# A retention block followed by a low-rank mixer and MLP: the first MLP layer of the last two tiles partly as seven half-size products

## The chip, the cores and the metric

The kernel runs on one core of a Trainium2 chip. The metric is the device time of one execution in microseconds; the time of a kernel is the median of several executions. TensorE (PE in the profile) multiplies matrices into PSUM, VectorE (DVE) and ScalarE (ACT) read PSUM and work element by element, GpSimd (POOL) works on SBUF only, SyncE (SP) and POOL issue transfers.

## The reference

Eight sequences of 576 tokens go through a retention (linear attention with a decay per head, 8 heads of 64), and its output `x` (8 x 576 x 512) through a token mixer of rank 32 and an MLP of width 2048:

```python
scores = scale * np.matmul(q, k.transpose(0, 1, 3, 2))
ret = scores * Dmat[None]                     # gamma_h ** (i - j) for i >= j, else 0
x = np.matmul(ret, v)                         # heads side by side: (8, 576, 512)
h = x.transpose(0, 2, 1) @ U @ V
u = x + h.transpose(0, 2, 1)
out = u + np.maximum(u @ w_ch1, 0.0) @ w_ch2  # w_ch1: 512 x 2048, w_ch2: 2048 x 512
```

Only `np.maximum(u @ w_ch1, 0.0)`, the first layer, is what the change touches.

## The kernel before

The 4608 tokens are cut into nine tiles of 512 for the MLP. While tile j goes through the MLP, the retention and the mixer of sequence j+1 are worked in between its pieces; tiles 7 and 8, the last two, have nothing beside them, since the sequences have run out. Each engine executes its instructions in the order in which the program issues them (every engine object is wrapped in `Pinned`, which keeps program order), so a waiting instruction holds up all that stands behind it on its engine.

`mlp_units(j)` gives a tile's pieces, called units, and they are issued in order.

The first layer has 16 units, one for each of the `NF` blocks of 128 rows of the hidden layer. `first(f)` takes a PSUM bank from `ps_mm` (three banks in turn) and issues four matmuls of 128 x 512 that add up over the 512 inputs: weights from `w1_sb`, moving data from `ring["uT"]`, the transposed `u` of the tile's four chunks of 128 tokens. `relu(f)` on ACT writes the bank as bf16 into `y1` (16 blocks x 512 tokens). From tile 2 on the blocks are visited in the order 0, 8, 1, 9, ..., so that a block of the first half (`f < 8`) and its partner in the second half come together.

The second layer of tiles 2 to 8 is already done in seven products of half size (Strassen's scheme in Winograd's form), 14 units of eight matmuls of 128 x 256 each: `products` lists them, `product(n, half)` issues them. `quarter(i, fh)` is the part of `y1` with token half `i` and hidden half `fh`. The scheme needs sums of the quarters (`sum_up`, `difference`, `last_sum`, all on DVE, into `y1_sums` or in place) and sums of the quarters of the second weight (`w2_sums`, made once). `GROUPS` says after which units of the first layer `sum_up` takes two blocks of each half. The products share three PSUM banks "a", "b" and "c", taken from the same `ps_mm`. The functions `after_1`, `after_6`, ... add the products up and add `u`: `after_1` copies bank "a" on ACT; `after_6` adds bank "b" on DVE and then issues three additions of `u` on POOL, the first of which makes the output quarter `22` and the second the quarter `21`; `after_7` adds banks "b" and "c" to quarter `22`, stores it, and calls `last_sum`; `after_2` adds `u` to bank "a" on DVE and stores; `after_4` and `after_3` add banks "b" and "c" to the last two quarters. Product number 5 (counted from 0) adds onto bank "b" that `after_7` has read, and product number 6 reads what `last_sum` wrote.

The loop that issues all tiles but the first ends so:

```python
for n, unit in enumerate(units1 if j == 1 else mlp_units(j)[0]):
    while steps and steps[0][0] <= n:
        steps.pop(0)[2]()
    if j > 1 or n >= 3:
        unit()
for s in steps:
    s[2]()
```

Buffers that are no longer used in the last two tiles are the retention's: `k_sets` and `v_sets` (three each), `q_raw` (two), and the PSUM pools `banks["one"]` (three banks, tag "att") and `banks["two"]` (one buffer of two banks, tag "pss").

Of the kernel before, what the change touches and what calls it, by code (L numbers as in the profile page):

```python
# [8 lines left out]
FP32 = mybir.dt.float32  # L9
BF16 = mybir.dt.bfloat16  # L10
AF = mybir.ActivationFunctionType
ALU = mybir.AluOpType
# [55 lines left out]
def kernel(  # L68
# [12 lines left out]
    pe = Pinned(tc, nc.tensor)  # L81
    dve = Pinned(tc, nc.vector)
    act = Pinned(tc, nc.scalar)
# [6 lines left out]
    R = moe_U.shape[1]  # L90
    P = 128
# [4 lines left out]
    NF = dff // P  # L96
# [5 lines left out]
    NT = B * S // 512  # L102
# [19 lines left out]
    CH = 64  # L122
# [12 lines left out]
    ps_mm = ctx.enter_context(tc.tile_pool(name="ps_mm", bufs=3, space=bass.MemoryType.PSUM))  # L135
    banks = {}
# [6 lines left out]
    q_raw = [consts.tile([P, NR_COLS], BF16, name=f"q_all{i}") for i in range(NQ)]  # L143
# [15 lines left out]
    k_sets = [consts.tile([P, NB, H, D], BF16, name=f"k_all{i}") for i in range(NSET)]  # L159
    v_sets = [consts.tile([P, NB, H, D], BF16, name=f"v_all{i}") for i in range(NSET)]  # L160


    HF, HD = NF // 2, dm // 2
# [41 lines left out]
    w1_sb = consts.tile([P, NCC, dff], BF16, name="w1_sb")  # L205
# [94 lines left out]
    def clear_pads(b):  # L300
        m, pad = (NB - 1, slice(HALF, P)) if b % 2 == 0 else (0, slice(0, HALF))
        for x in (k_sets, v_sets):
            pool.memset(x[b % NSET][pad, m, :, :], 0.0)
# [245 lines left out]
    def mix_turn_by_dma(a, n):  # L549
# [8 lines left out]
    ring = {  # L558
        "u": consts.tile([P, NRING, dm], BF16, name="u_t"),
        "uT": consts.tile([P, NRING, NCC, P], BF16, name="uT_t"),  # L560
    }
# [351 lines left out]

    GROUPS = {4: (0, 2), 8: (2, 4), 12: (4, 6), 15: (6, 8)}

    def sums_of_w2(part):

        f = slice(part * HF // 2, (part + 1) * HF // 2)
        (b11, b12), (b21, b22) = (
            [w2_sb[:, fh * HF:(fh + 1) * HF, q * HD:(q + 1) * HD][:, f, :] for q in range(2)]  # L920
            for fh in range(2)
        )
        t3, t2, t4 = (w2_sums[:, i, f, :] for i in range(3))
        for to, x, y, op in (
            (t3, b22, b12, ALU.subtract), (t2, t3, b11, ALU.add), (t4, b21, t2, ALU.subtract),
        ):
            dve.tensor_tensor(out=to, in0=x, in1=y, op=op)

    def last_sum_of_w2(part):
        f = slice(part * HF // 2, (part + 1) * HF // 2)  # L930
        x = w2_sb[:, 0:HF, HD:dm][:, f, :]
        dve.tensor_tensor(out=x, in0=x, in1=w2_sb[:, 0:HF, 0:HD][:, f, :], op=ALU.subtract)

    def mlp_units(j):
        held = {}
# [6 lines left out]
        own = 4 * j % NRING  # L942
        sums = j >= 2
        order = [f for i in range(HF) for f in (i, i + HF)] if sums else list(range(NF))

        def relu(f):
            act.activation(out=y1()[:, f, :], in_=held.pop(f), func=AF.Relu)
# [10 lines left out]
        def first(f):  # L958
            held[f] = ps = ps_mm.tile([P, 512], FP32, tag="mm", name="ps_y1")
            for cc in range(NCC):  # L960
                pe.matmul(
                    ps, w1_sb[:, cc, f * P:(f + 1) * P], ring["uT"][:, own:own + 4, cc, :],
                    start=(cc == 0), stop=(cc == NCC - 1),
                )

        def second(i, part):
            if part == 0:
                held["out", i] = ps_mm.tile([P, 512], FP32, tag="mm", name="ps_y2")
            for f in range(4 * part, 4 * part + 4):
                pe.matmul(  # L970
                    held["out", i], y1()[:, f, i * P:(i + 1) * P], w2_sb[:, f, :],
                    start=(f == 0), stop=(f == NF - 1),
                )

        def add_and_store(i):
            o_sb = osb_pool.tile([P, dm], FP32, tag="o_sb", name="o_sb")
            dve.tensor_tensor(
                out=o_sb, in0=held.pop(("out", i)), in1=ring["u"][:, own + i, :], op=ALU.add
            )
            t0 = (4 * j + i) * P  # L980
            sp.dma_start(out=out.rearrange("b s d -> (b s) d")[t0:t0 + P, :], in_=o_sb)
# [19 lines left out]
        def sum_up(a, z):  # L1001

            f = slice(a, z)
            s1, s2 = (y1_sums[:, i, f, :] for i in range(2))
            dve.tensor_tensor(
                out=s1, in0=quarter(1, 0)[:, f, :], in1=quarter(1, 1)[:, f, :], op=ALU.add
            )
            dve.tensor_tensor(out=s2, in0=s1, in1=quarter(0, 0)[:, f, :], op=ALU.subtract)

        def difference(a, z):  # L1010
            f = slice(a, z)
            x = quarter(1, 0)[:, f, :]
            dve.tensor_tensor(out=x, in0=quarter(0, 0)[:, f, :], in1=x, op=ALU.subtract)
# [78 lines left out]
        def product(n, half):  # L1092
            bank, fresh, left, right, after = products[n]
            if bank not in held and rows_apart(bank):
                held[bank] = [
                    banks["one"].tile([P, 2, HD], FP32, tag="att", name="ps_y2") for _ in range(2)
                ]
            if bank not in held:
                held[bank] = ps_mm.tile([P, 2, HD], FP32, tag="mm", name="ps_y2")
            apart = rows_apart(bank)  # L1100
            for f in range(HF):
                pe.matmul(
                    bank_rows(bank, half), left()[:, f, half * P:(half + 1) * P],
                    right()[:, f, :], start=(fresh and (apart or half == 0) and f == 0),
                    stop=(f == HF - 1), skip_group_check=True,
                )
            if j == NT - 1 and after is after_3:
                after_3_rows(half)
            elif half == 1 and after:
                after()  # L1110

        def unit(n, alone=True):

            i, part = divmod(n - NF, 4)
            if n < NF:
                first(order[n])
            elif sums:
                product(*divmod(n - NF, 2))
            else:
                second(i, part)  # L1120
            if alone and n < NF:
                relu(order[n])
                if sums and n in GROUPS:
                    sum_up(*GROUPS[n])
                if sums and n == NF - 1:
                    difference(0, HF // 2)
                    difference(HF // 2, HF)
            elif alone and part == 3 and not sums and not (j == 1 and i in (1, 2)):
                add_and_store(i)

        steps = {"y": ahead, "R": relu, "M": lambda n: unit(n, False), "O": add_and_store}
        return [lambda n=n: unit(n) for n in range(NF + (14 if sums else 16))], steps


# [128 lines left out]
    n = 16  # L1263
    while n < SP:
        m = min(n, SP - n)
        dve.tensor_scalar(
            out=iota_col[:, n:n + m], in0=iota_col[:, 0:m], scalar1=float(n), scalar2=None,
            op0=ALU.add,
# [7 lines left out]
    for h in range(H):  # L1276
# [6 lines left out]
        out=ident, in_=ident, compare_op=ALU.not_equal, fill=1.0, base=0,  # L1283
# [13 lines left out]
    for i in range(2):  # L1297
# [7 lines left out]
        out=maskbin, in_=maskbin, compare_op=ALU.is_ge, fill=0.0, base=0,  # L1305
# [27 lines left out]
    for h in range(H):  # L1333
        dve.tensor_scalar(
            out=masks[:, h, :, :], in0=mask64, scalar1=float(gammas[h] ** -CH), scalar2=None,
            op0=ALU.mult,
# [6 lines left out]
            tc.tile_pool(name="ps_" + name, bufs=n, space=bass.MemoryType.PSUM))  # L1343


    for j in range(1, NT):
        if j == 1:
            clear_pads(4)
        steps = []
        if j == 1:  # L1350
            steps = sorted(
                attention_steps(2, (5, 8.5, 12, 15.5, 21), 1.5, 22, 8) + late
                + [(at, 3, lambda i=i: sums_of_w2(i)) for i, at in enumerate((3.2, 21.5))],
                key=lambda s: s[:2]
            )
        elif j + 1 < B:
            last = 17 if j < 5 else 16
            steps = attention_steps(j + 1, (-1.5, 2.5, 6.5, 10.5, last), 1.5, last + 1.8)
        if j == 2:
            steps += [(at, 3, lambda i=i: last_sum_of_w2(i)) for i, at in enumerate((2, 3))]  # L1360
        if 1 < j and j + 2 < B:
            wait_for_turns(j)
            load_for_turns(j + 2)
            if j + 3 < B:
                clear_pads(j + 3)
        if j + 2 < B:
            at = 22 if j == 1 else 20
            steps += [(at + h, 4, lambda h=h: scale_head(j + 2, h)) for h in range(H)]
        steps.sort(key=lambda s: s[:2])
# [4 lines that stand above are left out]
                unit()  # L1374
        for s in steps:
            s[2]()

# [28 lines left out]
```

## Time and profile before

| | |
|---|---|
| median of three executions | 314.66 us (313.89 to 316.91) |
| the profiled execution | 315.51 us, its span 313.8 us |
| granted TensorE clock | 0.993 |
| PE busy | 305.6 us, 97% of the span |
| DVE busy | 229.0 us, 73% |
| ACT busy | 166.8 us, 53% |
| POOL busy | 131.3 us, 42% |

A profile describes one execution; its time beyond the span (1.7 us here) lies before the first and after the last instruction. The timeline view lists, by start, how long a merged run of equal instructions lasted, on which engine, output <- inputs, shapes, count, and in brackets the idle time of the engine just before it with what ended it. The view of groups gives count, total busy time and mean duration in ns. Every instruction carries line L25, the helper's, so it is told apart by the names of its tiles: `ps_y` is any PSUM bank of the MLP, `w_sb` both weights, `uT_t` the transposed `u`, `y_t` the hidden layer, `y_sums` its sums, `kv_runs` the sums of the second weight, `o_sb` an output quarter on its way to memory. PE durations include the drain of the pipeline, so the rate of matmuls is read from the distances of their starts.

### The profile page before, as it was taken

The page shows a single profiled execution, that of the slowest core. Times are in us where ns is not written, and L with a number is a line of the kernel's source. Part 1 is how long each engine was busy: PE and PEld are TensorE (multiplying, and loading weights), DVE is VectorE, ACT ScalarE, POOL GpSimd, SP SyncE. Part 2 cuts the span into 40 slices and gives each one's busy share as a digit, 9 for nine tenths or more (in the row PEclk, how much of TensorE's full clock was granted, in tenths as well). Part 3 has the DMA queues.
Part 4 walks back from the last instruction along what each step waited for, and adds up shares of the span by engine and source line. Part 5 has one row for each costly group of instructions (what it writes and reads, how often), then busy time and mean ns, then how long its engine had stood idle before and what let it go on. Part 6 is the DMA issues. An engine that isn't in the chain of part 4 may idle for free.

```text
span 313.8 us, 9434 instructions
## 1 busy us (share of the span) xinstructions
PE 305.6 (97%) x3937; PEld 190.9 (61%) x3952; DVE 229.0 (73%) x562; ACT 166.8 (53%) x346; POOL 131.3 (42%) x171
## 2 busy tenths in 40 slices
PE   8799999999999999999999999999999999999995
PEld 3575446745544557855784578457845784685484
DVE  6776818877988997899688968996799772352245
ACT  7556605447725775377437745774377406604610
POOL 8492258849302952259439612961200120040040
PEclk9979999999999999999999999999999999999999
DMA  7999999999995999799999994999910052002003
GB/s 117 193 182 198 204 212 145 170 184 133 173 123 162 158 113 146 118 157 148 154 210 162 143 148 119 178 139 118 212 56 4 3 131 86 2 33 102 0 2 135
DMA packets 154523, 40.58 MB, mean 129 GB/s; under 512 B 139088, under 2 KB 153456, under 8 KB 154480
## 3 DMA queue, kind: packets, MB, share of 16 engines
q0 software_dynamic: 91344, 17.09, 71.7%
q1 hardware_dynamic: 63136, 22.88, 40.9%
q8 instruction: 31, 0.51, 0.7%
q14 instruction: 12, 0.10, 0.1%
HBM read 36.85 MB, written 9.44 MB: 147 GB/s over the span
## 4 chain that ended last, share of the span: by engine, by line
PE 84%; DVE 7%; DMA 4%; issue 2%; SPq 1%; ACT 0%; POOL 0%; DVEq 0%; POOLq 0%
PE ps_y L25 69%; PE xh L25 5%; PE ps_b L25 4%; DMA given<-in_v_dram 2%; DMA kv_runs<-in_v_dram 2%; PE sc L25 2%; SPq L25 1%; PE pss L25 1%; DVE u_t L25 1%; PE ps_h L25 1%; PE ps_at L25 1%; DVE v_all L25 1%; DVE S L25 1%; DVE V_sb L25 1%; DVE qT_all L25 1%
## 5 line engine op out<-in xcount | busy, mean ns | idle before, releaser
L25 PE MATMUL ps_y<-uT_t,w_sb 128*128 128x512 bf16 x576 | 130.3, 379 | 0.2
L25 ACT ACTIVATE y_t<-ps_y 128x512 bf16<-128x512 f32 x144 | 85.6, 597 | 59.6 <-PE ps_y L25 58.5
L25 PEld LDWEIGHTS <-w_sb 128*128 128x128 bf16 x576 | 54.4, 98 | 61.5 <-issue 0.4
L25 POOL TENSOR_TENSOR o_sb<-o_sb,u_t 128x512 f32<-128x512 f32 x21 | 23.9, 1152 | 104.8 <-DVE o_sb L25 100.3
L25 PEld LDWEIGHTS <-y_t 128*128 128x128 bf16 x576 | 55.2, 98 | 18.9
L25 PE MATMUL ps_y<-w_sb,y_t 128*128 128x256 bf16 (+1 forms) x345 | 56.4, 310 | 0.5 <-issue 0.2
L25 DVE SCALAR_TENSOR_TENSOR S<-S,keep,pss 128x64 bf16<-128x64 bf16 x168 | 47.0, 280 | 6.0 <-ACT S L25 0.9
L25 DVE TENSOR_TENSOR o_sb<-ps_y,o_sb 128x512 f32<-128x512 f32 (+1 forms) x37 | 24.4, 662 | 26.6 <-PE ps_y L25 12.8
L25 DVE TENSOR_TENSOR ret<-sc,qsrow 128x640 bf16<-128x640 f32 x48 | 39.2, 819 | 2.5 <-PE sc L25 2.2
L25 PEld LDWEIGHTS <-y_sums 128*128 128x128 bf16 x336 | 32.0, 98 | 5.2 <-issue 0.5
L25 POOL DMA_DIRECT2D k_all<-in_k_dram x36 | 30.1, 853 | 8.2 <-DMA w_sb<-in_moe_w_ch_dram 8.2
L25 POOL DMA_DIRECT2D q_all<-in_q_dram x37 | 29.3, 801 | 5.5 <-DMA w_sb<-in_moe_w_ch_dram 4.2
L25 ACT ACTIVATE v_all<-v_all,vs 128x320 bf16<-128x320 bf16 x40 | 18.7, 548 | 22.1 <-DMA v_all<-in_v_dram 20.8
L25 DVE TENSOR_TENSOR y_sums<-y_t 128x512 bf16<-128x512 bf16 x28 | 11.8, 420 | 22.1 <-ACT y_t L25 22.1
L25 POOL DMA_DIRECT2D v_all<-in_v_dram x31 | 26.5, 918 | 2.4 <-DMA k_all<-in_k_dram 1.6
L25 PE MATMUL ps_y<-w_sb,y_sums 128*128 128x256 bf16 x224 | 27.4, 273 | 0.1
L25 PE MATMUL ps_y<-kv_runs,y_t 128*128 128x256 bf16 x224 | 26.9, 273 | 0.2
L25 ACT ACTIVATE x_t<-xh,xs 128x320 bf16<-128x320 f32 x48 | 22.7, 523 | 7.4 <-PE xh L25 5.8
L25 DVE TENSOR_TENSOR u_t<-ps_h,x_t 128x512 bf16<-128x512 f32 (+2 forms) x39 | 22.4, 629 | 2.5 <-PE ps_h L25 2.3
L25 POOL COPY landed<-uT_t 128x4 bf16<-128x4 bf16 (+3 forms) x5 | 0.9, 188 | 38.4 <-DMA uT_t<-u_t 38.4
L25 PE MATMUL ps_y<-kv_runs,y_sums 128*128 128x256 bf16 x112 | 14.1, 273 | 0.3 <-issue 0.3
L25 PEld LDWEIGHTS <-ret 128*128 128x128 bf16 (+1 forms) x320 | 11.8, 98 | 2.5 <-issue 0.2
(133 smaller groups left out, 297.0 us busy)
## 6 DMA issues: line engine op xcount, KB each, us to landing
out_dram<-o_sb SPq DMA_DIRECT2D x35, 256.0 KB, 2.6
w_sb<-in_moe_w_ch_dram POOLq DMA_DIRECT2D x8, 512.0 KB, 12.1
v_all<-in_v_dram POOLq DMA_DIRECT2D x25, 128.0 KB, 10.8
k_all<-in_k_dram POOLq DMA_DIRECT2D x24, 128.0 KB, 6.3
q_all<-in_q_dram POOLq DMA_DIRECT2D x20, 128.0 KB, 4.8
q_all<-in_q_dram POOLq DMA_DIRECT2D x12, 144.0 KB, 6.0
given<-in_v_dram SPq DMA_DIRECT2D x8, 128.0 KB, 5.5
kv_runs<-in_v_dram SPq DMA_DIRECT2D x3, 256.0 KB, 6.0
```

The lines of the kernel that those rows point to most:

```text
L25: return self._tc.keep_in_program_order(call(*args, **kwargs))
```

## The change

The last two tiles leave the loop (`for j in range(1, NT - 2)`) and are issued by a new function, `last_tiles`, in an order written out by hand. In them the hidden blocks are taken in groups of two blocks of each half (group g: blocks 2g, 2g+1, 8+2g, 9+2g). A group is four units of the first layer before. In groups 1 and 2 of tile 7 and groups 0, 1 and 2 of tile 8, the four units are replaced by seven products of half size, `seventh(n, g)`, each of four matmuls of 128 x 256. The other three groups, 0 and 3 of tile 7 and 3 of tile 8, stay as they were.

The seven products need four sums of weight quarters, S1 to S4 (`sum_of_w1`, for the blocks concerned, into `k_sets` and `v_sets`) and four sums of `u` quarters, T1 to T4 (`sum_of_u`). They run on DVE: those of tile 7 at its start, those of tile 8 behind the fourth unit of tile 7's second layer, right behind `after_6`. Three partial results of a group (after products 1, 6 and 7, all in one bank "a") are copied by ACT to SBUF as f32 (`shares`, in `q_raw`). Three of the four quarters of the group's result are made on DVE (`finish`): an addition of a PSUM bank and such a copy, written as bf16, and then a maximum with 0 in place. The fourth is a relu on ACT. Products 5 and 3 of a group share a bank of `banks["one"]`, product 2 takes half of `banks["two"]`, and product 3 may start only when `finish` of product 5 has read the bank. The first two products of tile 8 are issued around the last product of tile 7's second layer, where they take the bank of `ps_mm` that `after_2` reads.

The diff, shortened:

```diff
+    def sum_of_w1(n, a, z):
+        f = slice(a * P, z * P)
+        (a11, a12), (a21, a22) = ([w1_quarter(i, c)[:, :, f] for c in range(2)] for i in range(2))
+        s1, s2, s3, s4 = (x[:, :, f] for x in w1_sums)
+        to, x, y, op = (
+            (s1, a21, a22, ALU.add), (s2, s1, a11, ALU.subtract),
+            (s3, a11, a21, ALU.subtract), (s4, a12, s2, ALU.subtract),
+        )[n]
+        dve.tensor_tensor(out=to, in0=x, in1=y, op=op)
...
-                if sums and n in GROUPS:
+                if sums and n in GROUPS and (j < NT - 2 or n == NF - 1):
                     sum_up(*GROUPS[n])
...
+        def sum_of_u(n):
+            (b11, b12), (b21, b22) = ([u_quarter(i, t) for t in range(2)] for i in range(2))
...
+            to, x, y = ((t1, b12, b11), (t2, b22, t1), (t3, b22, b12), (t4, b21, t2))[n]
+            dve.tensor_tensor(out=to, in0=x, in1=y, op=ALU.subtract)
+
+        def seventh(n, g):
+            f = slice(2 * g, 2 * g + 2)
+            kept = shares[g % 2]
...
+            bank, left, right = {
+                1: ("a", w(0, 0), u(0, 0)), 6: ("a", summed(1), u_sum(1)),
+                7: ("a", summed(2), u_sum(2)), 4: ("a", w(1, 1), u_sum(3)),
+                5: ("c", summed(0), u_sum(0)), 3: ("c", summed(3), u(1, 1)),
+                2: ("d", w(0, 1), u(1, 0)),
+            }[n]
...
+            for i in range(2):
+                for c in range(2):
+                    pe.matmul(
+                        ps[:, i, :], left(c)[:, (2 * g + i) * P:(2 * g + i + 1) * P], right(c),
+                        start=(fresh and i == 0 and c == 0), stop=(c == 1),
+                        skip_group_check=True,
+                    )
+
+            def finish(i, fh, share):
+                y = quarter(i, fh)[:, f, :]
+                dve.tensor_tensor(out=y, in0=ps, in1=kept[:, share], op=ALU.add)
+                dve.tensor_scalar(out=y, in0=y, scalar1=0.0, scalar2=None, op0=ALU.max)
+
+            if n in (1, 6, 7):
+                act.copy(out=kept[:, (1, 6, 7).index(n)], in_=ps)
...
+            if n in (5, 7) and done >= {5, 7}:
+                ps = held["L", g, "c"]
+                finish(1, 1, 2)
+            elif n == 4:
+                act.activation(out=quarter(0, 1)[:, f, :], in_=ps, func=AF.Relu)
+            elif n == 2:
+                finish(0, 0, 0)
+            elif n == 3:
+                finish(1, 0, 1)
+                sum_up(2 * g, 2 * g + 2)
...
-    for j in range(1, NT):
+    def last_tiles():
+        (units, one), (last_units, two) = (mlp_units(j) for j in (NT - 2, NT - 1))
+        for i in range(4):
+            if i < 2:
+                one["sum_of_u"](i)
+                sum_of_w1(i, 2, 6)
+            else:
+                sum_of_w1(i, 2, 6)
+                one["sum_of_u"](i)
+        for n in range(3):
+            units[n]()
+        one["seventh"](1, 1)
+        units[3]()
+        for n, g in ((6, 1), (2, 1), (5, 1), (7, 1)):
+            one["seventh"](n, g)
+        one["sum_up"](0, 2)
+        for n, g in ((1, 2), (2, 2), (4, 1), (6, 2), (5, 2), (3, 1), (7, 2)):
+            one["seventh"](n, g)
+        for n, x in zip(range(12, NF), (4, 3, None, None)):
+            units[n]()
+            if x:
+                one["seventh"](x, 2)
+        for n in range(NF, NF + 12):
+            units[n]()
+            if n == NF + 3:
+                for i in range(4):
+                    two["sum_of_u"](i)
+                    sum_of_w1(i, 0, 2)
+        for x, n in ((1, 12), (6, 13)):
+            two["seventh"](x, 0)
+            units[NF + n]()
+        for n, g in (
+            (7, 0), (2, 0), (5, 0),
+            (1, 1), (2, 1), (4, 0), (6, 1), (5, 1), (3, 0), (7, 1),
+            (1, 2), (2, 2), (4, 1), (6, 2), (5, 2), (3, 1), (7, 2),
+        ):
+            two["seventh"](n, g)
+        for n, x in zip(range(12, NF), (4, 3, None, None)):
+            last_units[n]()
+            if x:
+                two["seventh"](x, 2)
+        for n in range(NF, NF + 14):
+            last_units[n]()
+
+    for j in range(1, NT - 2):
...
+    last_tiles()
```

More of the change, by code (lines that the diff above doesn't have):

```diff
@@ L914, with flat, w1_quarter @@
     GROUPS = {4: (0, 2), 8: (2, 4), 12: (4, 6), 15: (6, 8)}
+    def flat(x):
+        return x.rearrange("p c h d -> p (c h d)")
+    w1_sums = [
+        flat(x)[:, 0:2 * HF * P].rearrange("p (c f) -> p c f", c=2)
+        for x in (k_sets[2], v_sets[2], k_sets[0], v_sets[0])
+    ]
+    u_sums = [
+        flat(x)[:, 0:8 * 2 * P].rearrange("p (i c t) -> p i c t", i=4, c=2)
+        for x in (k_sets[1], v_sets[1])
+    ]
+    shares = [
+        x.bitcast(FP32)[:, 0:3 * 512].rearrange("p (n f t) -> p n f t", n=3, f=2) for x in q_raw
+    ]
+    def w1_quarter(i, c):
+        return w1_sb[:, 2 * c:2 * c + 2, i * HF * P:(i + 1) * HF * P]
+    def sum_of_w1(n, a, z):
[7 more added lines that the diff above has]
+        dve.tensor_tensor(out=to, in0=x, in1=y, op=op)
     def sums_of_w2(part):
@@ L1129, in unit, with u_quarter @@
                 add_and_store(i)
-        steps = {"y": ahead, "R": relu, "M": lambda n: unit(n, False), "O": add_and_store}
+        def u_quarter(i, t):
+            return ring["uT"][:, own + 2 * t:own + 2 * t + 2, 2 * i:2 * i + 2, :]
+        def sum_of_u(n):
+            (b11, b12), (b21, b22) = ([u_quarter(i, t) for t in range(2)] for i in range(2))
+            t1, t2, t3, t4 = (
+                u_sums[j % 2][:, i].rearrange("p c (h t) -> p h c t", h=2) for i in range(4)
+            )
+            to, x, y = ((t1, b12, b11), (t2, b22, t1), (t3, b22, b12), (t4, b21, t2))[n]
+            dve.tensor_tensor(out=to, in0=x, in1=y, op=ALU.subtract)
@@ new lines, in seventh, with w, summed, u @@
+        def seventh(n, g):
+            f = slice(2 * g, 2 * g + 2)
+            kept = shares[g % 2]
+            def w(i, c):
+                return lambda x: w1_quarter(i, c)[:, x]
+            def summed(i):
+                return lambda x: w1_sums[i][:, x]
+            def u(i, t):
+                return lambda x: u_quarter(i, t)[:, :, x, :]
+            def u_sum(i):
+                return lambda x: u_sums[j % 2][:, i, x, :]
+            bank, left, right = {
[4 more added lines that the diff above has]
+            }[n]
+            fresh = n in (1, 5, 2)
+            if n == 1:
+                held["L", g, "a"] = ps_mm.tile([P, 2, 2 * P], FP32, tag="mm", name="ps_y1")
+            elif n == 5:
+                held["L", g, "c"] = banks["one"].tile(
+                    [P, 2, 2 * P], FP32, tag="att", name="ps_y1")
+            elif n == 2:
+                if "two" not in held:
+                    held["two"] = banks["two"].tile([P, 2, 8, CH], FP32, tag="pss", name="ps_y1")
+                held["L", g, "d"] = held["two"][:, g % 2].rearrange("p (f x) t -> p f (x t)", f=2)
+            ps = held["L", g, bank]
+            for i in range(2):
[4 more added lines that the diff above has]
+                        skip_group_check=True,
+                    )
+            def finish(i, fh, share):
[4 more added lines that the diff above has]
+                act.copy(out=kept[:, (1, 6, 7).index(n)], in_=ps)
+            done = held.setdefault(("L", g), set())
+            done.add(n)
+            if n in (5, 7) and done >= {5, 7}:
[3 more added lines that the diff above has]
+                act.activation(out=quarter(0, 1)[:, f, :], in_=ps, func=AF.Relu)
+            elif n == 2:
+                finish(0, 0, 0)
+            elif n == 3:
+                finish(1, 0, 1)
+                sum_up(2 * g, 2 * g + 2)
@@ L1132, in mlp_units @@
+        steps = {
+            "y": ahead, "R": relu, "M": lambda n: unit(n, False), "O": add_and_store,
+            "sum_of_u": sum_of_u, "seventh": seventh, "sum_up": sum_up,
+        }
         return [lambda n=n: unit(n) for n in range(NF + (14 if sums else 16))], steps
```

## The prediction

> **What bounds the kernel now.** I read the page's busy times first, then the chain that ended last, then the timeline of tiles 7 and 8.
>
> ```profile
> PE 305.6 (97%) x3937; PEld 190.9 (61%) x3952; DVE 229.0 (73%) x562; ACT 166.8 (53%) x346; POOL 131.3 (42%) x171
> 250.19 60.12 PE ps_y L25 x424
> 310.33 0.42 DVE o_sb L25
> ```
>
> From 250.19 us the chain is 60 us of MLP matmuls without a break, one last addition and the store. So a matmul that goes away shortens the end by its own time, and a wait of PE lengthens it by as much. One tile, from the timeline, PE first:
>
> ```profile
> 258.05 13.98 PE L25 MATMUL ps_y<-uT_t,w_sb 128*128 128x512 bf16 x64
> 271.86 1.91 PE L25 MATMUL ps_y<-w_sb,y_t 128*128 128x256 bf16 x16
> 275.35 1.91 PE L25 MATMUL ps_y<-w_sb,y_sums 128*128 128x256 bf16 x16
> 278.85 1.91 PE L25 MATMUL ps_y<-w_sb,y_t 128*128 128x256 bf16 x16
> 280.59 1.91 PE L25 MATMUL ps_y<-kv_runs,y_t 128*128 128x256 bf16 x16
> 282.34 1.91 PE L25 MATMUL ps_y<-w_sb,y_sums 128*128 128x256 bf16 x16
> 284.09 13.98 PE L25 MATMUL ps_y<-uT_t,w_sb 128*128 128x512 bf16 x64
> ```
>
> The first layer's 64 matmuls take 271.86 - 258.05 = 13.81 us, 215.8 ns each; the second layer's 112 of half width 284.09 - 271.86 = 12.23 us, 109.2 ns each. Half a width costs half the time, weight loads included. DVE, ACT and POOL of the same tile:
>
> ```profile
> 258.32 0.69 DVE L25 TENSOR_TENSOR o_sb<-ps_y,o_sb 128x512 f32<-128x512 f32 x1 [1.07 <-PE ps_y L25]
> 259.97 0.60 ACT L25 ACTIVATE y_t<-ps_y 128x512 bf16<-128x512 f32 x1 [0.22 <-PE ps_y L25]
> 262.33 0.43 DVE L25 TENSOR_TENSOR y_sums<-y_t 128x512 bf16<-128x512 bf16 x1 [3.32 <-ACT y_t L25]
> 262.79 0.42 DVE L25 TENSOR_TENSOR y_sums<-y_sums,y_t 128x512 bf16<-128x512 bf16 x1
> 273.49 1.28 DVE L25 TENSOR_TENSOR y_t<-y_t 128x1024 bf16<-128x1024 bf16 x2
> 275.61 0.69 DVE L25 TENSOR_TENSOR o_sb<-ps_y,o_sb 128x512 f32<-128x512 f32 x1 [0.83 <-issue]
> 276.38 3.50 POOL L25 TENSOR_TENSOR o_sb<-o_sb,u_t 128x512 f32<-128x512 f32 x3 [23.20 <-DVE o_sb L25]
> 279.10 1.42 DVE L25 TENSOR_TENSOR o_sb<-ps_y,o_sb 128x512 f32<-128x512 f32 x2 [2.80 <-PE ps_y L25]
> 280.44 1.22 DVE L25 TENSOR_TENSOR y_sums<-y_t,y_sums 128x2048 bf16<-128x2048 bf16 x1
> 281.57 0.69 DVE L25 TENSOR_TENSOR o_sb<-ps_y,u_t 128x512 f32<-128x512 f32 x1
> ```
>
> These give the rules for the walk below. DVE follows PE by 0.26 us (matmuls over at 275.35, DVE at 275.61), ACT by 0.20 (the eight matmuls of units 0 and 1 over at 258.05 + 8 x 0.2158 = 259.78, relu at 259.97). An operation that needs the one before it on DVE starts 0.03 after its end (262.33 + 0.43, 262.79); one that doesn't starts 0.09 before (two of 0.684 in 1.28). PE follows DVE by 0.05 (11.49 + 0.06, 11.60):
>
> ```profile
> 11.49 0.06 DVE L25 MEMSET given<- 128x2 f32 x1
> 11.60 0.21 PE L25 MATMUL ps_b<-v_all,ret 64*128 64x64 bf16 x2 [0.22 <-DVE given L25]
> ```
>
> **Prices of the new work**, from the groups of the whole trace:
>
> ```profile
> L25 DVE TENSOR_TENSOR o_sb<-ps_y,o_sb 128x512 f32<-128x512 f32 x33 | 22.8, 691 | 26.0 <-PE ps_y L25 12.2 <-ACT at_diag L25 7.4 <-issue 6.1
> L25 DVE TENSOR_TENSOR y_sums<-y_sums,y_t 128x512 bf16<-128x512 bf16 x28 | 11.9, 425 | 1.0
> L25 DVE TENSOR_TENSOR y_t<-y_t 128x1024 bf16<-128x1024 bf16 x14 | 9.0, 684 | 0.0
> L25 DVE COPY V_sb<-V_sb 32x576 bf16<-32x576 bf16 x7 | 1.9, 298 | 0.1
> L25 DVE COPY mask<-maskbin 128x128 bf16<-128x128 bf16 x1 | 0.1, 131 | 0.0
> L25 ACT ACTIVATE y_t<-ps_y 128x512 bf16<-128x512 f32 x144 | 85.6, 597 | 59.6 <-PE ps_y L25 58.5
> L25 ACT COPY o_sb<-ps_y 128x512 f32<-128x512 f32 x7 | 4.1, 586 | 4.4 <-PE ps_y L25 4.2
> ```
>
> An addition of `finish` is PSUM f32 plus SBUF f32, 0.69 us. Its maximum in place, bf16 with one source, has no row of its shape: below, the copy of 128 elements at 0.13; above, the two-source operation at 0.425; I take 0.29, by the nearest row, one source and 576 elements at 0.298. Sums of 512 elements cost 0.425, of 1024 0.684, copies on ACT 0.59.
>
> **Step 1, matmuls removed.** A group was 16 x 215.8 ns = 3.45 us and becomes 28 x 109.2 = 3.06: 0.395 less, for five groups **-1.98 us**. That is all that the change can gain.
>
> **Step 2, sums at tile 7's start: nothing.** Behind the addition at 258.32 DVE makes T and S in 4 x (0.425 - 0.09) + 4 x (0.684 - 0.09) = 3.7 us, from 258.9 to 262.8. Product 6 needs the first four, there by 261.0; PE reaches it at 261.98, behind units 0 to 3 and product 1 (258.05 + 4 x 0.863 + 0.437, and 0.04 for ACT's copy). Without that cover it would wait up to 2 us.
>
> **Step 3, the groups: DVE falls behind.** A group puts three `finish` and one `sum_up` on DVE: 3 x (0.69 + 0.29) + 2 x 0.425 = 3.8 us, some 3.6 with the overlaps, against 3.06 of PE; on ACT 3 x 0.59 + 0.60 = 2.4, which PE's other products hide but for some 0.1 us in all.
>
> Tile 7. On PE products 6, 2, 5 and 7 of group 1 (0.437 each) run from 261.98 to 263.73. ACT's copy of the last follows from 263.93 to 264.51, and at 264.54 DVE goes on: `finish` (0.69 + 0.03 + 0.29 - 0.09 = 0.93), `sum_up` (0.80), `finish` of group 2 (0.93), `finish` of product 3 of group 1 (1.05, as the sum behind it depends on it), `sum_up` (0.80), and the addition (0.69) that frees the bank for product 3 of group 2: over at 269.7. PE gets to that product after seven products (3.06), unit 12 (0.86), product 4 (0.44) and unit 13 (0.86): 263.73 + 5.22 = 268.95. It waits 0.8, and behind it on PE stand units 14 and 15 and the second layer, for which ACT's relus and the sums wait.
>
> Tile 8 has one group more. Counted from the end of its first product 3 on PE, DVE starts 0.26 later and needs 1.05 + 0.80 + 0.93 + 0.93 + 1.05 + 0.80 + 0.69 = 6.25 to the same addition, 6.5 in all; PE needs eight products, units 12 and 13 and product 4: 3.50 + 1.73 + 0.44 = 5.67. It waits 0.8, some 0.2 of it already before product 3 of group 1. With ACT's 0.1 the two tiles lose **+1.7 us**. The two queues hold three and four maxima: at 0.13 each the waits come to 0.6, at 0.425 to 2.7. The second layer's first sums then come no later than before, as the last `sum_up` waits for unit 15's relu in both kernels.
>
> **Step 4, sums for tile 8 in tile 7's second layer.** They go into DVE's idle time between 276.30 and 279.10: eight operations of 0.425 - 0.09, done at 279.07. By that they would just fit. But POOL's three additions lie in the same place (276.38 to 279.88). DVE's work beside POOL's additions in this kernel reads PSUM and only one SBUF operand, and costs nothing; the new sums read two SBUF operands. That pair occurs once in the trace:
>
> ```profile
> 17.36 1.10 POOL L25 TENSOR_TENSOR v_all<-given,vscale 128x512 bf16<-128x512 f32 x1
> 17.61 1.41 DVE L25 TENSOR_TENSOR v_all<-given,vscale 128x512 bf16<-128x512 f32 x1
> L25 DVE TENSOR_TENSOR v_all<-given,vscale x3: 682/682/1405, 7.9 to 17.6; 128x512 bf16<-128x512 f32 x3
> 249.52 3.20 DVE L25 TENSOR_TENSOR u_t<-ps_h,x_t 128x512 bf16<-128x512 f32 x5
> 249.68 3.50 POOL L25 TENSOR_TENSOR o_sb<-o_sb,u_t 128x512 f32<-128x512 f32 x3 [27.77 <-DVE o_sb L25]
> ```
>
> DVE's operation of 0.68 us took 1.41 when POOL was at work for 0.85 us of it: 0.72 more, nearly the whole overlap, where half speed would have cost 0.43. It ended 0.55 after POOL, so it began in earnest 0.13 before POOL's end. The last two lines are the counter-example: five additions from PSUM beside POOL, 0.64 apart, none held up.
>
> The Trainium skill (SBUF — State Buffer, Who interferes with whom) says the same more widely: a VectorE instruction with two SBUF inputs and a GpSimd instruction that reads SBUF exclude each other for the whole instruction, whoever started first. This trace agrees in its one instance, f32; that it holds for bf16 sums and in the other direction no row shows. By the page all three additions of POOL would stand between the sums.
>
> By half speed for DVE alone, the row's other reading, the sums would end 1.7 us late instead of 3.1, and the total come to about +1.2; I take the full block, as the row is nearer to it.
>
> Walk, with POOL's and DVE's operations in turn: T1 to 276.7, POOL to 277.8, S1 to 278.1, POOL to 279.2, T2 to 279.5, POOL to 280.5, S2 to 280.8, the last four to 282.2. `after_7`, ready at 279.10, starts at 282.15: first addition to 282.84. Product 5 adds onto the bank it reads and starts at 282.89 instead of 280.66 (280.59 and 0.07 from steps 1 to 3): 2.2 us, and product 6 and all of tile 8 are queued behind. It ends at 284.64; the second addition, `last_sum` and `after_2` (0.69, 1.22, 0.69 with overlaps) end at 285.3, and tile 8's first product, which takes the bank `after_2` has read, waits another 0.7. **+2.9 us.** The bounds are 0, if nothing is held up, and 2.9; if DVE's eight run through and POOL comes after them (from 279.0), the first quarter is ready at 280.15, product 5 waits 0.3, `last_sum` waits for POOL until 282.4, and tile 8's first product 1.5: 1.8.
>
> **Step 5, the rest: nothing.** Nothing moves past SP or the DMAs; stores go out as much later as their additions. The last tile's end (310.33 and the store) is unchanged.
>
> **Sum.** -1.98 + 1.7 + 2.9 = +2.6 us on the profiled execution's 315.51 (span 313.8 and 1.7 around it), 318.1. The median, 314.66, lies 0.85 lower; on it: **317.3 us**.
>
> **Rivals.** (A) the forecast, 55 in 100: 317.3; by the price of the maximum 316.2 to 318.3. (B) DVE's burst first, then POOL: +1.5, 316.2. For it: DVE starts an operation 0.09 before the last one's end, leaving POOL little room; against: each has some 0.16 us beside its 0.27 of streaming (425 ns for 512 elements, 684 for 1024), in which POOL, waiting since 276.38, can get in. 20 in 100. (C) The other side: POOL and the sums run side by side. Step 4 is then free, and the sum is -1.98 + 1.7 = -0.3: 314.4. It decides at `after_7`, whose slack is 0.03 us: sums done by 279.1, no loss. For it: they are bf16 and half as long as the one held-up row, which is single; against: that row. 20 in 100; with a fast maximum 313.3. (D) Over 318.3: an ordering edge between quarters of one block of `y_t` that the code doesn't need, or a dear maximum on top of A. 5 in 100. That the seven products aren't faster on PE I exclude: the second layer runs the same form at 109.2 ns.
>
> **How the numbers follow.** About 1%, 3.15 us, is what a measurement of this kernel can tell from no change. Faster by that is out of reach of -1.98: 1 in 100. Slower by that starts at 317.8: the upper third of A, and D: 22. Within: 77. The range leaves out the lower part of C and the upper part of D: 314.1 to 318.4.
>
> **What would show it.** PE 109 ns apart in the groups (step 1); idle PE of 0.5 to 1 us before product 3 of the last group in each tile, put down to DVE's `y_t` (step 3); the maximum near 0.29 us. In tile 7's second layer single DVE sums of 1.2 to 1.6 us instead of 0.425 among POOL's additions, PE idle some 2.2 us before product 5 and 0.7 before tile 8's first product (step 4). Wrong: sums of 0.425 beside POOL with PE unbroken there (C), POOL's first addition late or three times as long (B), or idle PE where the walk has none.

## The result

The changed kernel takes 0.85% longer: the ratio to the kernel before is 1.0085, 95% interval 1.0061 to 1.0109, some 2.7 us; medians of 21 executions 317.81 and 315.01 us. The forecast was 317.3 on a median of 314.66, a ratio of 1.0084.

The profiled execution of the changed kernel has a span of 319.6 us and was disturbed ahead of tile 7: it starts that tile at 261.38 us instead of 258.05, after code that is the same in both kernels. So all profiles below, in all of which the granted clock over that stretch is 1.00, are compared by a length **L** that leaves this out: from tile 7's first matmul of the first layer to the end of the last addition, 310.33 + 0.42 - 258.05 = **52.70 us before** and 316.12 + 0.42 - 261.38 = **55.16 us after**, 2.46 more. L is read from one profiled execution of each kernel; the ratios compare the whole times of several.

A second remark on reading: the idle time of PE in brackets runs from the modelled end of a matmul, 0.16 us behind the place where the next one could start. The waits in this text are distances of starts, so 0.16 more than the brackets.

Tile 7's first layer in the timeline of the changed kernel (`q_all` holds the copies, `k_all` and `v_all` the sums of weights and `u`):

```profile
261.38 4.05 PE L25 MATMUL ps_y<-uT_t,w_sb 128*128 128x512 bf16 x20
265.29 0.60 PE L25 MATMUL ps_y<-v_all,v_all 128*128 128x256 bf16 x4
266.16 1.04 PE L25 MATMUL ps_y<-v_all,k_all 128*128 128x256 bf16 x8
267.03 1.04 PE L25 MATMUL ps_y<-uT_t,w_sb 128*128 128x256 bf16 x8
267.85 0.69 DVE L25 TENSOR_TENSOR y_t<-ps_y,q_all 128x512 bf16<-128x512 f32 x1 [0.42 <-ACT q_all L25]
268.58 0.29 DVE L25 TENSOR_SCALAR y_t<-y_t 128x512 bf16<-128x512 bf16 x1
272.36 0.68 DVE L25 TENSOR_TENSOR y_t<-ps_y,q_all 128x512 bf16<-128x512 f32 x1
273.09 0.60 PE L25 MATMUL ps_y<-uT_t,v_all 128*128 128x256 bf16 x4 [0.67 <-DVE y_t L25]
275.25 1.91 PE L25 MATMUL ps_y<-w_sb,y_t 128*128 128x256 bf16 x16
```

Eight matmuls of a group take 267.03 - 266.16 = 0.87 us, 109 ns each, as forecast. Yet the layer lasts 275.25 - 261.38 = 13.87 us, 0.06 more than the 13.81 before: two groups save 0.79, and PE loses that and 0.06 more, nearly all in one place, before product 3 of group 2, where it stands still for 0.83 until DVE's addition (272.36 to 273.04) has read the bank.

The second layer of tile 7, in the same view:

```profile
279.00 0.69 DVE L25 TENSOR_TENSOR o_sb<-ps_y,o_sb 128x512 f32<-128x512 f32 x1 [0.83 <-issue]
279.61 0.42 DVE L25 TENSOR_TENSOR k_all<-uT_t 128x512 bf16<-128x512 bf16 x1
279.77 3.86 POOL L25 TENSOR_TENSOR o_sb<-o_sb,u_t 128x512 f32<-128x512 f32 x3 [23.25 <-DVE o_sb L25]
279.94 1.38 DVE L25 TENSOR_TENSOR k_all<-w_sb 128x512 bf16<-128x512 bf16 x1
281.24 1.37 DVE L25 TENSOR_TENSOR k_all<-uT_t,k_all 128x512 bf16<-128x512 bf16 x1
282.24 1.91 PE L25 MATMUL ps_y<-w_sb,y_t 128*128 128x256 bf16 x16
282.54 1.37 DVE L25 TENSOR_TENSOR v_all<-k_all,w_sb 128x512 bf16<-128x512 bf16 x1
283.84 0.41 DVE L25 TENSOR_TENSOR k_all<-uT_t 128x512 bf16<-128x512 bf16 x1
285.18 1.40 DVE L25 TENSOR_TENSOR o_sb<-ps_y,o_sb 128x512 f32<-128x512 f32 x2
285.91 1.91 PE L25 MATMUL ps_y<-kv_runs,y_t 128*128 128x256 bf16 x16 [1.76 <-DVE o_sb L25]
288.36 0.60 PE L25 MATMUL ps_y<-uT_t,w_sb 128*128 128x256 bf16 x4 [0.55 <-DVE o_sb L25]
```

Of the eight sums the first takes 0.42 us, the next three 1.37 to 1.38, the last four 0.41. The three long ones are the number of POOL's additions, which last 3.86 us together instead of 3.50: the two engines take turns. So `after_7` starts at 285.18, 2.7 us after product number 3 of the second layer (counted from 0, as all products of that layer) allows it (PE done at 282.24, and 0.25). The second layer's product number 5 stands still for 285.91 - 282.24 - 1.75 = 1.92 us, and tile 8's first product another 288.36 - 285.91 - 1.75 = 0.70.

PE's waits on DVE in this stretch, in the view of waits:

```profile
PE ps_y L25 <- DVE o_sb L25: 2.3, 2, 1.8
PE ps_y L25 <- DVE y_t L25: 1.1, 2, 0.7
```

The books close: -1.98 from the matmuls, +1.92 + 0.70 in tile 7's second layer, +0.85 in the groups of tile 7 (13.87 against 13.81 - 0.79 = 13.02) and +0.95 in those of tile 8 (its first layer and the rest of product 6 need 14.38 us at the rates above and last from 288.36 to 303.69). The sum is +2.44; L grew by 2.46.

### The profile page after: what moved, and what is told of

The parts are those of the page before. It is cut to its first block, busy times and chain, and to the rows that moved or that the text cites. A ratio compares the mean times of both kernels' runs of the same rounds, so it can differ in the third digit from the quotient of the medians.

```text
span 319.6 us, 9643 instructions
## 1 busy us (share of the span) xinstructions
PE 307.2 (96%) x4012; PEld 197.5 (62%) x4012; DVE 251.6 (79%) x608; ACT 165.8 (52%) x346; POOL 131.8 (41%) x171
## 4 chain that ended last, share of the span: by engine, by line
PE 85%; DVE 8%; DMA 3%; issue 1%; ACT 1%; POOL 0%; SPq 0%; DVEq 0%; POOLq 0%; ACTq 0%
PE ps_y L25 69%; PE ps_b L25 5%; PE xh L25 5%; DMA given<-in_v_dram 3%; DVE y_t L25 2%; PE sc L25 2%; DVE S L25 1%; PE ps_h L25 1%; PE pss L25 1%; DVE y_sums L25 1%; DVE v_all L25 1%; PE ps_at L25 1%; DVE o_sb L25 1%; ACT v_all L25 1%; DVE qT_all L25 1%
## 5 line engine op out<-in xcount | busy, mean ns | idle before, releaser
L25 PE MATMUL ps_y<-uT_t,w_sb 128*128 128x512 bf16 (+1 forms) x536 | 119.3, 371 | 0.6 <-DVE o_sb L25 0.6
L25 ACT ACTIVATE y_t<-ps_y 128x512 bf16<-128x512 f32 x129 | 76.3, 597 | 46.5 <-PE ps_y L25 45.5
L25 PEld LDWEIGHTS <-w_sb 128*128 128x128 bf16 x556 | 52.5, 98 | 53.0 <-issue 1.1
L25 PE MATMUL ps_y<-w_sb,y_t 128*128 128x256 bf16 (+1 forms) x352 | 57.6, 312 | 0.0
L25 PEld LDWEIGHTS <-k_all 64*64 64x64 bf16 (+2 forms) x604 | 14.1, 110 | 5.4 <-issue 4.1
L25 ACT COPY q_all<-ps_y 128x512 f32<-128x512 f32 x15 | 8.6, 585 | 16.3 <-PE ps_y L25 16.3
```

The source lines that it names most:

```text
L25: return self._tc.keep_in_program_order(call(*args, **kwargs))
```

## The experiments

**1. The sums moved behind `after_2`.** Theory: POOL and DVE exclude each other. Rival: DVE has too much to do in this layer, wherever it is done.

```diff
-            if n == NF + 3:
+            if n == NF + 9:
                 for i in range(4):
                     two["sum_of_u"](i)
                     sum_of_w1(i, 0, 2)
```

> The changed kernel with the eight sums for tile 8 issued behind after_2 of tile 7's second layer (behind product 4, counted from 0) instead of behind after_6. Measure: L, from tile 7's first matmul to the end of the last addition; 52.70 us in the kernel before, 55.16 in the changed one. Collision theory (POOL's three additions and the sums, which read two SBUF operands, exclude each other): there POOL is done, each sum costs 0.42, both waits of PE in that layer go (1.92 + 0.71), L 52.5, ratio to before 0.999. Rival (DVE simply has 2.8 us too much to do in that layer): the delay moves to tile 8's first additions, L stays over 54.5, ratio 1.006 or more.

```profile
256.65 4.05 PE L25 MATMUL ps_y<-uT_t,w_sb 128*128 128x512 bf16 x20
275.05 3.50 POOL L25 TENSOR_TENSOR o_sb<-o_sb,u_t 128x512 f32<-128x512 f32 x3 [23.26 <-DVE o_sb L25]
279.26 1.91 PE L25 MATMUL ps_y<-kv_runs,y_t 128*128 128x256 bf16 x16
280.84 0.41 DVE L25 TENSOR_TENSOR k_all<-uT_t 128x512 bf16<-128x512 bf16 x1
281.01 0.60 PE L25 MATMUL ps_y<-uT_t,w_sb 128*128 128x256 bf16 x4
281.17 0.42 DVE L25 TENSOR_TENSOR k_all<-w_sb 128x512 bf16<-128x512 bf16 x1
308.80 0.42 DVE L25 TENSOR_TENSOR o_sb<-ps_y,o_sb 128x256 f32<-128x256 f32 x1 [0.38 <-PE ps_y L25]
```

The sums cost 0.42 each, POOL's additions are back to 3.50, and tile 8's first product follows product 5 by 281.01 - 279.26 = 1.75: no wait. L is 52.57, the ratio to before 0.9994 (0.9958 to 1.0029). The place of eight instructions was worth 2.6 us, and the rival falls. The new place fits exactly: the fourth sum, the last that tile 8's product 6 needs, ends at 282.27, and PE reaches that product at 282.32.

**2. POOL's additions out, the sums left in place.** The counter-trial, which changes POOL's work (and adds two copies on ACT) and leaves DVE's as it was.

```diff
             plus(held["12"], "b")
+            if j == NT - 2:
+                act.copy(out=new("22"), in_=held["12"])
+                act.copy(out=new("21"), in_=held["12"])
+                return
```

> The changed kernel; in tile 7 alone POOL's three additions of u are left out and two copies on ACT stand in their place, so three output quarters of tile 7 lack u. The sums stay where they were. Collision theory: all eight sums take 0.42 us, product 5 and tile 8's first product don't wait, L 52.5. Rival (DVE's load): sums as long in all as the slot, product 5 still waits over 1 us, L over 54.5. Half and half (ACT's copies hold them up as POOL did) would show sums of 0.8 to 1 us.

```profile
258.20 4.05 PE L25 MATMUL ps_y<-uT_t,w_sb 128*128 128x512 bf16 x20
276.77 0.42 DVE L25 TENSOR_TENSOR k_all<-w_sb 128x512 bf16<-128x512 bf16 x1
280.82 1.91 PE L25 MATMUL ps_y<-kv_runs,y_t 128*128 128x256 bf16 x16
310.35 0.42 DVE L25 TENSOR_TENSOR o_sb<-ps_y,o_sb 128x256 f32<-128x256 f32 x1 [0.38 <-PE ps_y L25]
```

All sums take 0.42 beside ACT's copies; L is 52.57, the same as in experiment 1. With DVE's load and its place unchanged, POOL's additions are what held the sums up.

**3. The sums alone, in the kernel before.** Nothing of the seven products, only eight sums of the same shapes behind `after_6` in tile 7.

```diff
             if j > 1 or n >= 3:
                 unit()
+            if j == NT - 2 and n == NF + 3:
+                extra_sums()
```

> The kernel before, with nothing of the change but eight sums of the same shapes behind after_6 in tile 7, whose results nobody reads. Collision theory: three of them take 1.38 us, product 5 starts 1.9 to 2.0 us late; the bank that after_2 reads isn't wanted until tile 8, and last_sum ends 0.1 us after product 5, so L 54.7 to 54.8, ratio to before 1.0065. Rival (the sums fit into DVE's idle time, the loss belongs to the seven products): L 52.7, ratio 1.000.

```profile
256.70 13.98 PE L25 MATMUL ps_y<-uT_t,w_sb 128*128 128x512 bf16 x64
275.04 3.85 POOL L25 TENSOR_TENSOR o_sb<-o_sb,u_t 128x512 f32<-128x512 f32 x3 [23.19 <-DVE o_sb L25]
275.20 1.38 DVE L25 TENSOR_TENSOR k_all<-w_sb 128x512 bf16<-128x512 bf16 x1
281.17 1.91 PE L25 MATMUL ps_y<-kv_runs,y_t 128*128 128x256 bf16 x16 [1.76 <-DVE o_sb L25]
311.03 0.42 DVE L25 TENSOR_TENSOR o_sb<-ps_y,o_sb 128x256 f32<-128x256 f32 x1 [0.38 <-PE ps_y L25]
```

L is 54.75, the ratio 1.0061 (1.0025 to 1.0096): the same 1.38 us sums and the same wait of 1.92 without any of the change's matmuls.

**4. The same eight sums behind `after_2`, in the kernel before.** The diff is that of experiment 3 with `NF + 9`.

> The kernel before with eight sums of the same shapes behind after_2 of tile 7, read by nobody. Collision theory: the place decides, not the work; each sum 0.42 us, PE waits nowhere, L 52.70. Rival (2.8 us more on DVE in that layer cost time wherever they stand): L over 53.5, since DVE has 1.1 us idle from there to the end of the layer and the first relus of tile 8 don't need it.

```profile
257.18 5.13 PE L25 MATMUL ps_y<-uT_t,w_sb 128*128 128x512 bf16 x23
283.99 1.28 DVE L25 TENSOR_TENSOR o_sb<-ps_y,o_sb 128x512 f32<-128x512 f32 x2
284.73 2.53 PE L25 MATMUL ps_y<-uT_t,w_sb 128*128 128x512 bf16 x11 [0.48 <-DVE o_sb L25]
310.10 0.42 DVE L25 TENSOR_TENSOR o_sb<-ps_y,o_sb 128x256 f32<-128x256 f32 x1 [0.38 <-PE ps_y L25]
```

A miss, between the two: L is 53.34. The sums cost 0.42 each and nothing in tile 7 waits, but they push the addition of `after_4` back to 283.99, and it reads the bank that unit 1 of tile 8 takes next: 0.64 us. In the changed kernel the second bank of tile 8 isn't wanted until five products later, so experiment 1 didn't meet this. "Nothing in the layer needs it" is not enough; the next owner of each bank has to be named.

**5. The maximum left out.** For the other loss, the groups: theory, DVE's load; rival, ACT's copies or the banks.

```diff
                 dve.tensor_tensor(out=y, in0=ps, in1=kept[:, share], op=ALU.add)
-                dve.tensor_scalar(out=y, in0=y, scalar1=0.0, scalar2=None, op0=ALU.max)
```

> The changed kernel without the maximum with 0 behind finish's additions, so three quarters of each group keep their negative values. Theory (DVE is 0.5 us a group short, and the maximum is 0.2 to 0.3 us of each finish): the waits before product 3 (0.67 and 0.48 in the changed kernel, 0.95 with the small ones in tile 8) go, L 53.5 to 53.7. Rival (those waits come from ACT's copies or from the banks, not from DVE's load): they stay above 0.5, L 54.9 to 55.2.

```profile
257.03 4.05 PE L25 MATMUL ps_y<-uT_t,w_sb 128*128 128x512 bf16 x20
PE ps_y L25 <- DVE o_sb L25: 2.3, 2, 1.8
310.22 0.42 DVE L25 TENSOR_TENSOR o_sb<-ps_y,o_sb 128x256 f32<-128x256 f32 x1 [0.38 <-PE ps_y L25]
```

The line of waits on `y_t` is gone, that on `o_sb` (the collision) is unchanged, and L is 53.61, 1.55 less than in the changed kernel and as expected. The groups wait for DVE.

**6. Both losses taken away**: experiments 1 and 5 together.

> The kernel with the sums behind after_2, and without the maximum with 0 behind finish's additions (three quarters of each group keep their negative values). If the two losses are all there is between the 1.98 us that the seven products save and what was measured, taking both away leaves L at 52.70 - 1.98 and some 0.1 to 0.2 of small waits on ACT: 50.8 to 50.9. Rival (half-width products cost more than their 109 ns in the groups, or a further wait lies behind these two): L over 51.3.

```profile
256.63 4.05 PE L25 MATMUL ps_y<-uT_t,w_sb 128*128 128x512 bf16 x20
283.94 1.29 DVE L25 TENSOR_TENSOR y_t<-ps_y,q_all 128x512 bf16<-128x512 f32 x2
284.11 1.18 PE L25 MATMUL ps_y<-uT_t,w_sb 128*128 128x256 bf16 x8
284.69 0.75 PEld L25 LDWEIGHTS <-w_sb 128*128 128x128 bf16 x7 [0.15 <-issue]
307.22 0.42 DVE L25 TENSOR_TENSOR o_sb<-ps_y,o_sb 128x256 f32<-128x256 f32 x1 [0.38 <-PE ps_y L25]
```

The view of waits has no wait of PE left in the last two tiles, and L is 51.01: 1.69 of the 1.98 us, 0.1 over the expected 50.8 to 50.9, and under the rival's 51.3. Of the other 0.29, some 0.13 are small gaps behind ACT's copies, as expected. About 0.14 lie in one place in tile 8 that the prediction's walk did not have. Products 1 and 2 of group 1 last 1.18 us there where eight such matmuls elsewhere last 1.04, and the idle 0.15 of the weight loads (PEld) falls ahead of product 2's second load. Just before, DVE's first addition, `finish` of product 2 of group 0, ends (283.94 + 0.69 = 284.63); it reads the other half of the same buffer of `banks["two"]`. The changed kernel loses 0.12 in the same place. That PE waits for this read is read off the order in time; no run tests it.

**7. Product 3 of the last group behind unit 14**, with the sums behind `after_2`: a way to keep the maximum.

```diff
-        for n, x in zip(range(12, NF), (4, 3, None, None)):
+        for n, x in zip(range(12, NF), (4, None, 3, None)):
```

> The sums behind after_2, and product 3 of the last group behind unit 14 instead of unit 13, in both tiles. DVE's queue then has 0.86 us more before PE asks for its bank: the waits of 0.67 and 0.48 go. But what follows that product on DVE (finish 1.05, sum_up 0.80, sum_up 0.80 behind the last relu) then ends some 0.4 us after the second layer's second product could start: two waits of 0.4 there, put down to y_sums. L 52.57 - 0.5 = 52.0 to 52.1, ratio to before 0.9975. Rival (DVE has room behind the first layer): L 51.3 to 51.5.

```profile
258.64 3.62 PE L25 MATMUL ps_y<-uT_t,w_sb 128*128 128x512 bf16 x18
272.88 0.42 DVE L25 TENSOR_TENSOR y_sums<-y_t 128x512 bf16<-128x512 bf16 x1
273.34 0.42 DVE L25 TENSOR_TENSOR y_sums<-y_sums,y_t 128x512 bf16<-128x512 bf16 x1
273.44 1.91 PE L25 MATMUL ps_y<-kv_runs,y_sums 128*128 128x256 bf16 x16
309.32 0.42 DVE L25 TENSOR_TENSOR o_sb<-ps_y,o_sb 128x256 f32<-128x256 f32 x1 [0.38 <-PE ps_y L25]
```

Better than either expected: L is 51.10, the ratio 0.9936 (0.9903 to 0.9968), faster than the kernel before and than the changed one. The waits on `y_t` are gone and the expected ones on `y_sums` didn't come. Product 1 of the second layer starts at 273.44 while the last sum is still at work until 273.76. It reads the hidden blocks in order, 0.109 us each, and needs that sum for its last two only. My 0.4 had charged the first matmul of the product with the last block's sum.

**8. One maximum of three on ACT**, product 3 where the change has it, sums behind `after_2`.

```diff
+        def late_relu(g):
+            y = quarter(1, 1)[:, 2 * g:2 * g + 2, :]
+            act.activation(out=y, in_=y, func=AF.Relu)
...
-                dve.tensor_scalar(out=y, in0=y, scalar1=0.0, scalar2=None, op0=ALU.max)
+                if (i, fh) != (1, 1):
+                    dve.tensor_scalar(out=y, in0=y, scalar1=0.0, scalar2=None, op0=ALU.max)
...
+            if n == 6 and ("L", g - 1) in held:
+                late_relu(g - 1)
...
```

> The sums behind after_2, product 3 where the change has it, and one maximum of each group's three (that of the quarter made after products 5 and 7) on ACT, behind the copy after product 6 of the next group or behind unit 13's relu, where ACT is idle 0.6 to 0.7 us. It takes 0.2 us a group off DVE's queue: the waits before product 3 shrink from 0.67 and 0.48 to some 0.35 and 0.15. L 51.9 to 52.0, ratio to before 0.997. Rival (ACT then comes late with the copies that PE needs): PE waits for q_all, L 52.5 or more.

```profile
255.88 4.05 PE L25 MATMUL ps_y<-uT_t,w_sb 128*128 128x512 bf16 x20
264.01 0.64 ACT L25 ACTIVATE y_t<-y_t 128x512 bf16<-128x512 bf16 x1
267.34 0.60 PE L25 MATMUL ps_y<-uT_t,v_all 128*128 128x256 bf16 x4 [0.41 <-DVE y_t L25]
307.59 0.42 DVE L25 TENSOR_TENSOR o_sb<-ps_y,o_sb 128x256 f32<-128x256 f32 x1 [0.38 <-PE ps_y L25]
```

L is 52.13, 0.1 to 0.2 over the expected 51.9 to 52.0; the ratio to before, 0.9983 (0.9960 to 1.0005), is not clear of no change. The wait shrank in the brackets from 0.67 to 0.41, where some 0.35 was expected, and ACT's 0.64 us stood in nobody's way. Moving the product (7) beats taking one maximum of three off the queue (8).

| kernel | L, us | ratio to before |
|---|---|---|
| before | 52.70 | 1 |
| changed | 55.16 | 1.0085 (1.0061 to 1.0109) |
| sums behind after_2 | 52.57 | 0.9994 (0.9958 to 1.0029) |
| POOL's additions out | 52.57 | one execution, no interval |
| before, with the sums | 54.75 | 1.0061 (1.0025 to 1.0096) |
| before, sums behind after_2 | 53.34 | one execution, no interval |
| maximum out | 53.61 | one execution, no interval |
| sums behind after_2, maximum out | 51.01 | one execution, no interval |
| sums behind after_2, product 3 later | 51.10 | 0.9936 (0.9903 to 0.9968) |
| sums behind after_2, one maximum on ACT | 52.13 | 0.9983 (0.9960 to 1.0005) |

## Why the prediction was right

Rival A, the forecast, is what happened, and the terms hold one by one. The time alone would not have shown it: the stated range, 314.1 to 318.4, also holds rival B's 316.2 and rival C's 314.4. The traces and the experiments decide between them.

Step 1, -1.98: half-width matmuls ran at 109 ns in the groups; with both losses removed 1.69 of it came out (experiment 6).

Step 2, nothing: tile 7's first product on sums started at 265.29, 3.91 us behind the first matmul, forecast 3.93; no wait.

Step 3, +1.7: measured 0.85 and 0.95. Additions 0.69, maximum 0.29, both at the price taken; the wait before product 3 of group 2 in tile 7 was 0.83 against 0.8, at the same product in tile 8 0.64 against 0.6. The 0.2 before product 3 of group 1 in tile 8 came to 0.09, and 0.12 came in a place where the walk had nothing (experiment 6). The price of the maximum was a choice by likeness, from a copy of 576 elements on 32 partitions; that it came out within 0.01 is in part luck, and by the prediction's own bounds of 0.13 and 0.425 it was worth some 2 us.

Step 4, +2.9: measured 2.62, the mechanism as walked, a little dear. I had let DVE and POOL take 1.4 us a turn; the sums start 1.30 apart (279.94, 281.24, 282.54, 283.84), 0.27 less than POOL's 1.15 and DVE's 0.42, each as undisturbed, laid end to end. Three turns make the 0.3 difference. Rival B falls to the order in the trace (POOL gets its turn after the very first sum), rival C to the three sums of 1.37 us and to experiments 1 to 3. That the one early collision (1.41 us, f32) would hold for bf16 sums half as long was a bet on one row; the runs bear it out.

The Trainium skill (SBUF — State Buffer, Who interferes with whom) has the rule that a VectorE instruction with two SBUF inputs and a GpSimd instruction reading SBUF exclude each other. These runs agree, 1.38 us against 0.42, and POOL's 3.86 against 3.50 shows the exclusion from the other side; the 0.27 us by which a pair is shorter than its parts shows that it doesn't cover the whole recorded durations. No run changed the operands of the sums: that it is the second SBUF operand rests on that rule and on the prediction's five additions from PSUM that POOL did not hold up.

Where my steps failed was in the experiments: in 6 and 8 L came out some 0.1 longer than expected, in 4 I overlooked the next owner of a PSUM bank (0.64), and in 7 I charged a product's first matmul with the last block's sum (0.4 in each tile).

## What to carry to other kernels

Before work goes into an engine's idle slot, look at what the other engines do in that slot: eight sums of 0.42 us fitted DVE's gap to 0.03 us and cost 2.6 because POOL was reading SBUF in it; in the changed kernel they cost nothing six units later, in the kernel before 0.64 (experiment 4). A saving on the bound engine is worth only what the followers can keep up with: a group saves 0.395 us on PE and puts three additions and maxima, some 2.8 us, more on DVE. Asking for the contested product later (experiment 7) got back 1.47 us, taking one maximum of three off the queue (experiment 8) 0.44. When a step is moved, list for each PSUM bank who takes it next, and which matmul of a product first needs the late data.

## What the runs showed of the hardware

I had not expected the turns to be so regular, or to overlap: with both queues filled, the starts and ends fit POOL and DVE alternating one instruction each, at 1.30 us a pair (1.57 if laid end to end, 1.15 and 0.42). POOL's stretch grows by only 0.36 us over three additions while DVE's grows by 2.9. So DVE, whose instructions are the shorter ones here, bears nearly all of the loss; whether the lengths decide that, no run shows.
